# Filler products on TensorE at the start, and batch 1's attention a unit later, in an attention-plus-MLP kernel

## The chip, the cores and the metric

One Trainium2 chip, one core of it, one launch. The time is device microseconds of that core, the median over several runs. Five engines work side by side and are tied by semaphores: TensorE (PE in the profile, its weight loads PEld), VectorE (DVE), ScalarE (ACT), GpSimd (POOL) and SyncE (SP), which issues most of the transfers.

## The reference, cut to what matters

```python
# q, k, v: 8 batches x 8 heads x 576 positions x 64, float32
q_s = exp(q - max(q, axis=-1));  q_s = q_s / (sum(q_s, axis=-1) + 1e-09)
k_s = exp(k - max(k, axis=2));   k_s = k_s / (sum(k_s, axis=2) + 1e-09)
kv  = einsum('bhsd,bhse->bhde', k_s, v)      # 64 x 64 per batch and head
x   = einsum('bhsd,bhde->bhse', q_s, kv)     # then as 4608 tokens x 512
h   = x @ w_in                               # 512 x 2048
out = maximum(0.01 * h, h) @ w_out           # 2048 x 512, float32 out
```

The softmax of q runs over the 64 channels of a position, that of k over the 576 positions of a channel.

## The kernel before, in words

**Two halves of the work.** The attention turns each of the 8 batches into 576 columns of `xT` (512 channels by 4608 tokens, bf16). The two matrix products then run over 9 tiles of 512 tokens: `layer1` (L450) makes 16 blocks of 128 hidden units (four products each, accumulated over the channel blocks in the order 0, 2, 1, 3), `leaky` (L460, ScalarE) writes them as `gj`, and `layer2` (L472) accumulates 16 of them into `pout`, one per 128 tokens; `store` (L465) copies `pout` to `out_sb` and issues two transfers.

**How the order is set.** Nothing is scheduled by a tool: every engine runs its instructions in the order in which the program text issues them. The main loops are cut into units: tile `t` has 16 units for its first layer (one per hidden block) and 16 for its second; tile 0 has 16 units for each half of its tokens in the first layer (0 to 31) and units 32 to 47 in the second layer, one per hidden block with four products each. `at(t, u, ...)` (L484) hangs attention work behind a unit, and `run(t, u)` (L489) issues it there. Batch 0 is done before the first tile; the rest of batch 0 and all of batch 1 hang in tile 0; batch 2 and later ones hang in the tiles that follow.

**The start.** Batch 0's q (rows `RA`, the first four positions of nine of each partition), k and v are loaded first. `wake(n)` (L322) issues n products of a zero tile, 128x512 bf16, into a PSUM bank that nobody reads; 14 of them open TensorE's order. `q_first` (L228) takes the negated maxima of q in two halves on VectorE (`nmax`), and ScalarE makes one exponential with a running sum per head and position. `k_tree` (L149) takes maxima of k on VectorE; `k_max_pe` (L328) transposes them on TensorE, `k_all_dve` reduces, `k_all_pe` (L342) spreads the result over all partitions, and `k_sub_ps` (L352) subtracts. This is done for two pairs of heads in turn, with dummies between the steps. ScalarE then casts v (`v_cast`), and `kv_pair` (L360) multiplies. Four more dummies, `q_transpose` (L386 on), the second `kv_pair`, `attend` (L408), three dummies and the first layer follow. The first weights, `w_in`, come in eight transfers issued by GpSimd (L133) in two groups of four, the second group behind batch 0's subtraction.

**Batch 1's end, in tile 0's second layer.** Behind unit 41 come `kv(1)`, `kd_make(1)` and the transposes of positions 0 to 3; behind unit 43 the transposes of positions 4 to 8, with ScalarE's copies out of PSUM (`q_keep`). Eight `attend` calls, four blocks of channels by two halves of 288 tokens, hang at units 45, 45, 46, 46, 46, 47, 47, 47; ScalarE copies each to `xT`. The four `store` calls of tile 0 are issued after the last unit's products and ahead of what hangs at unit 47 (L666). Tile 1's first layer needs batch 1's columns, and batch 2's maxima (`k_tree`, VectorE) hang at its unit 0, its subtraction at unit 6 and its exponential (ScalarE) at unit 9.

**PSUM.** Two banks hold `pout`; six more (`psB_pool`) are shared by all other tiles, among them the last two `pout2` of tile 0.

Of the kernel before, what the change touches and what calls it, by code (L numbers as in the profile page):

```python
# [8 lines left out]
FP32 = mybir.dt.float32  # L9
# [12 lines left out]
HL = 4  # L22
# [3 lines left out]
def kernel(  # L26
# [9 lines left out]
    nc = tc.nc  # L36
# [10 lines left out]
    P = 128  # L47
    NB = C // P
    NF = F // P
    TT = 512  # L50
    NT = T // TT
    NTS = TT // P
# [9 lines left out]
    small_pool = ctx.enter_context(tc.tile_pool(name="small", bufs=3))  # L62
# [23 lines left out]
    RA, RB = slice(0, 4), slice(4, R)  # L86
    R1, R2 = slice(4, 6), slice(6, R)
    st = [{} for _ in range(B)]
# [15 lines left out]
    identf = const_pool.tile([P, P], FP32)  # L104
# [44 lines left out]
    def k_tree(b, hs, steps=slice(0, 4)):  # L149
        n = hs.stop - hs.start  # L150
        ks = st[b]["k"][:, hs]
        if steps.start == 0:
            st[b]["t4"] = mx_pool.tile([P, HL, 4, D], FP32, name="t4")[:, 0:n]
        t4 = st[b]["t4"]
        t2, t1 = t4[:, :, 0:2], t4[:, :, 0]
        for o, i0, i1 in (
            (t4, ks[:, :, 0:4], ks[:, :, 4:8]),
            (t2, t2, t4[:, :, 2:4]),
            (t1, t1, t4[:, :, 1]),
            (st[b]["kmax"][:, hs], t1, ks[:, :, 8]),  # L160
        )[steps]:
            nc.vector.tensor_tensor(out=o, in0=i0, in1=i1, op=ALU.max)  # L162
# [55 lines left out]
    def q_begin(b):  # L218
        st[b]["qe"] = qe_pool.tile([P, R, HL, D], BF16, name="qe")
        if b < 2:  # L220
            st[b]["qT"] = qT_pool.tile([P, NB, R, L], BF16, name="qT", tag="qT")
# [6 lines left out]
    def q_first(b, rs):  # L228

        n = rs.stop - rs.start  # L230
        nmax = small_pool.tile([P, HL, n], FP32, name="nmax")
        qsum = small_pool.tile([P, n, HL], FP32, name="qsum")
        for hs in (slice(0, 2), slice(2, 4)):
            nc.vector.tensor_reduce(
                out=nmax[:, hs], in_=st[b]["q"][:, hs, rs], axis=AX.X, op=ALU.max, negate=True
            )
            for h in range(hs.start, hs.stop):
                for r in range(n):
                    nc.scalar.activation(
                        out=st[b]["qe"][:, rs.start + r, h],  # L240
                        in_=st[b]["q"][:, h, rs.start + r],
                        func=AF.Exp,
                        bias=nmax[:, h, r : r + 1],
                        accum_out=qsum[:, r, h : h + 1],
                    )
        st[b]["qsum"] = qsum
# [73 lines left out]
    wake_ps = psO_pool.tile([P, TT], FP32, name="pout")  # L320

    def wake(n):  # L322
        for i in range(n):
            nc.tensor.matmul(  # L324
                wake_ps, lhsT=zero[:, 0:P], rhs=zero, start=(i == 0), stop=(i == n - 1)
            )

    def k_max_pe(b, i):  # L328
        ps = psB_pool.tile([P, 2, L], FP32, name="kT", tag=BANK_TAG)
        nc.tensor.matmul(  # L330
            ps.rearrange("c h l -> c (h l)"),
            lhsT=st[b]["kmax"][:, 2 * i : 2 * i + 2].rearrange("p h d -> p (h d)"),
            rhs=identf,
            is_transpose=True,
        )
        st[b]["kT", i] = ps
# [5 lines left out]
    def k_all_pe(b, i):  # L342
        ps = psB_pool.tile([P, P], FP32, name="kallp", tag=BANK_TAG)
        for hh in range(2):
            nc.tensor.matmul(
                ps[hh * L : (hh + 1) * L],
                lhsT=st[b]["kr", i][:, hh : hh + 1].to_broadcast([P, L]),
                rhs=identf,
            )
        st[b]["kallp", i] = ps  # L350

    def k_sub_ps(b, i, hs=slice(0, 2)):  # L352
        ks = st[b]["k"][:, 2 * i + hs.start : 2 * i + hs.stop]
        a = st[b]["kallp", i].rearrange("p (h d) -> p h d", d=D)[:, hs]
        n = hs.stop - hs.start
        nc.vector.tensor_tensor(
            out=ks, in0=ks, in1=a.unsqueeze(2).to_broadcast([P, n, R, D]), op=ALU.subtract
        )
# [26 lines left out]
    def q_transpose(b, r0, n):  # L385
        ps = psB_pool.tile([P, NB, n, L], BF16, name="psum_qt", tag=BANK_TAG)  # L386
        for rr in range(n):
            for gg in range(2):
                nc.tensor.matmul(  # L389
                    ps[:, gg::2, rr],  # L390
                    lhsT=st[b]["qe"][:, r0 + rr, 2 * gg : 2 * gg + 2].rearrange(
                        "p h d -> p (h d)"
                    ),
                    rhs=ident,
                    is_transpose=True,
                    start=(rr == 0 and gg == 0),
                    stop=(rr == n - 1 and gg == 1),
                )
        st[b]["ps", r0] = ps

    def q_keep(eng, b, r0, n, gs=slice(0, 4)):
        o, i = st[b]["qT"][:, gs, r0 : r0 + n], st[b]["ps", r0][:, gs]
        if eng is nc.scalar:
            eng.copy(out=o, in_=i)
        else:
            eng.tensor_copy(out=o, in_=i)

    def attend(b, gs, c0, n, eng):  # L408

        ps = psB_pool.tile([P, len(gs), n], FP32, name="po", tag=BANK_TAG)  # L410
        for i, g in enumerate(gs):
            nc.tensor.matmul(  # L412
                ps[:, i],
                lhsT=kd2[b % 2][:, g],
                rhs=st[b]["qT"][:, g].rearrange("c r l -> c (r l)")[:, c0 : c0 + n],
                start=True,
                stop=True,
            )
        step = gs[-1] - gs[0] if len(gs) == 2 else 1
        o = xT[:, gs[0] : gs[-1] + 1 : step, b * S + c0 : b * S + c0 + n]  # L420
        if eng is nc.scalar:
            eng.copy(out=o, in_=ps)  # L422
        else:
            eng.tensor_copy(out=o, in_=ps)
# [40 lines left out]
    def store(row0, pout, copy=nc.vector.tensor_copy, os=slice(0, O), issue=(nc.sync, nc.sync)):  # L465
        out_sb = osb_pool.tile([P, O], FP32, name="out_sb")[:, os]
        copy(out=out_sb, in_=pout)  # L467
        for i in range(2):
            b, c = divmod(row0 + i * L, S)
            issue[i].dma_start(out=out_r[b, c // L, :, os], in_=out_sb[i * L : (i + 1) * L])  # L470

    def layer2(pout, g_sb, tsub, j, os=slice(0, O)):  # L472
        nc.tensor.matmul(  # L473
            pout,
            lhsT=g_sb[j // 2][:, j % 2, tsub * P : (tsub + 1) * P],
            rhs=w_out_sb[:, j, os],
            start=(j == 0),
            stop=(j == NF - 1),
        )
# [4 lines left out]
    def at(t, u, *fns):  # L484
        while t > 0 and u >= 32:
            t, u = t + 1, u - 32
        hooks.setdefault((t, u), []).extend(fns)

    def run(t, u):  # L489
        for fn in hooks.pop((t, u), ()):  # L490
            fn()

    H0, H1 = slice(0, 2), slice(2, 4)
    GS = (0, 2, 1, 3)
# [12 lines left out]

    HA, HB = slice(0, 1), slice(1, 2)
    wake(14)
    nc.gpsimd.tensor_copy(out=gate[:, 0:1], in_=st[0]["k"][:, HL - 1, R - 1, D - 1 : D])  # L510
    load_w_in(0)
    k_begin(0)
    q_begin(0)
    q_first(0, RA)
    k_tree(0, H0)
    k_max_pe(0, 0)
    wake(1)
    k_tree(0, H1, slice(0, 1))
    k_all_dve(0, 0)
    k_all_pe(0, 0)  # L520
    wake(2)
    k_tree(0, H1, slice(1, 4))
    k_max_pe(0, 1)
# [2 lines left out]
    k_exp(0, slice(0, 1))  # L526
    k_all_dve(0, 1)
    k_all_pe(0, 1)
    wake(2)
    k_sub_ps(0, 0, HB)  # L530
    k_exp(0, slice(1, 2))
    v_cast(nc.scalar, 0, 0)
# [56 lines left out]
    for r0 in (0, 2):  # L589
        at(0, 41, lambda r0=r0: q_transpose(1, r0, 2), lambda r0=r0: q_keep(nc.scalar, 1, r0, 2))  # L590
    for r0, n in ((4, 3), (7, 2)):
        at(0, 43, lambda r0=r0, n=n: q_transpose(1, r0, n), lambda r0=r0, n=n: q_keep(nc.scalar, 1, r0, n))
    for i in range(8):
        at(0, (45, 45, 46, 46, 46, 47, 47, 47)[i], lambda i=i: attend(1, [GS[i // 2]], 288 * (i % 2), 288, nc.scalar))


    XR = (slice(0, 5), slice(5, R))
# [63 lines left out]
    pout = [psO_pool.tile([P, O], FP32, name="pout") for _ in range(2)]  # L661
    pout += [psB_pool.tile([P, O], FP32, name="pout2", tag=BANK_TAG) for _ in range(2)]
    for j in range(NF):
        for tsub in range(NTS):
            layer2(pout[tsub], g_sb, tsub, j)
        if j == NF - 1:  # L666
            for tsub in range(NTS):
                store(tsub * P, pout[tsub])
        run(0, 32 + j)

    for t in range(1, NT):
        g_sb = []
# [54 lines left out]
```

## Time and profile before

| | us |
|---|---|
| median of 3 runs | 294.86 (294.04 to 294.93) |
| the profiled execution | 294.82, of it span 293.0 |
| TensorE busy in the span | 282.1 |
| VectorE, ScalarE, GpSimd busy | 145.6, 150.7, 85.4 |
| TensorE's clock halved | 13.59 to 17.01 |

Times in the profile are microseconds from the start of the span. A row of the timeline gives start, length, engine, line of the kernel, operation, output and inputs, partitions by elements and type, count, and in brackets the idle time of the engine ahead of it with what ended it. A product's length contains the way through the array, so products that follow one another overlap in such rows; their distance is read from the starts. The chain of waits is followed back from the last instruction and names at each step what released it. Line numbers are those of the kernel before.

### The profile page before, as it was taken

Reading aid. Unit: us, or ns where it says so; the run is one execution under the profiler, and the core shown is the slowest. Engines: PE = TensorE matmul, PEld = TensorE weight load, DVE = VectorE, ACT = ScalarE, POOL = GpSimd, SP = SyncE. Lnnn points to the kernel's source line nnn. Section 1 sums busy time; section 2 is a strip of 40 time slices with the busy share of each in tenths; the row PEclk is TensorE's granted clock in tenths of the full one; section 3 lists DMA queues with packets and bytes.
Section 4 is the critical chain, followed back from the end, with each engine's and each line's share of the span. In section 5 each row is a group of like instructions: output and inputs, shape, how many; then the busy total and the mean of one; then the engine's idle time right before and its main releaser. Section 6 shows DMA issues by size and latency. Waiting matters only on the chain.

```text
span 293.0 us, 4282 instructions
## 1 busy us (share of the span) xinstructions
PE 282.1 (96%) x1661; PEld 139.9 (48%) x1661; DVE 145.6 (50%) x240; ACT 150.7 (51%) x272; POOL 85.4 (29%) x61
## 2 busy tenths in 40 slices
PE   8698999999999999999999999999999999999995
PEld 2266845444544455454445544544455444444443
DVE  3946958696592597189367455735440200110011
ACT  4937684678058605951695338532854066007500
POOL 4645190008019307802930292029300000000000
PEclk9989999999999999999999999999999999999999
DMA  7999999496639553774399138933141310131032
GB/s 257 312 216 391 243 181 401 112 287 258 114 76 310 211 116 90 272 266 89 71 309 292 36 72 282 281 74 72 38 81 38 72 36 1 38 72 36 0 72 74
DMA packets 36580, 45.76 MB, mean 156 GB/s; under 512 B 15952, under 2 KB 19280, under 8 KB 36560
## 3 DMA queue, kind: packets, MB, share of 16 engines
q1 hardware_dynamic: 33120, 41.16, 47.9%
q0 software_dynamic: 3280, 4.20, 8.2%
q8 instruction: 13, 0.21, 0.3%
q10 hardware_dynamic: 160, 0.13, 0.1%
q14 instruction: 7, 0.06, 0.1%
HBM read 36.70 MB, written 9.44 MB: 157 GB/s over the span
## 4 chain that ended last, share of the span: by engine, by line
PE 85%; DVE 6%; POOL 2%; ACT 2%; issue 1%; POOLq 0%
PE pout L473 39%; PE ph L452 39%; PE pkv L295 2%; PE po L440 2%; DVE qe L280 1%; DVE qsum L273 1%; POOL k_raw L195 1%; DVE t L162 1%; PE pout L324 1%; PE psum_qt L389 1%; POOL q_raw L256 1%; PE po L412 1%; ACT xT L422 1%; PE pkv L365 1%; ACT qe L264 1%
## 5 line engine op out<-in xcount | busy, mean ns | idle before, releaser
L473 PE MATMUL pout<-w_out_sb,gj 128*128 128x512 bf16 (+2 forms) x592 | 130.4, 373 | 0.0
L452 PE MATMUL ph<-xT,w_in_sb 128*128 128x512 bf16 (+1 forms) x640 | 127.5, 358 | 1.6 <-ACT xT L422 1.6
L461 ACT ACTIVATE gj<-ph 128x512 bf16<-128x512 f32 x144 | 82.3, 604 | 58.1 <-PE ph L452 57.5
L452 PEld LDWEIGHTS <-w_in_sb 128*128 128x128 bf16 x640 | 62.1, 98 | 63.6 <-issue 2.9
L473 PEld LDWEIGHTS <-gj 128*128 128x128 bf16 x592 | 57.0, 98 | 61.8
L467 DVE COPY out_sb<-pout 128x512 f32<-128x512 f32 (+1 forms) x34 | 22.7, 675 | 90.3 <-PE pout L473 84.7
L195 POOL TENSOR_TENSOR k_raw<-k_raw,kall 128x2304 f32<-128x2304 f32 (+1 forms) x6 | 29.1, 4845 | 85.6 <-DVE kall L187 56.9
L256 POOL TENSOR_TENSOR q_raw<-q_raw,qmax 128x2304 f32<-128x2304 f32 (+4 forms) x11 | 31.1, 2836 | 25.8 <-DVE qmax L226 25.8
L273 DVE TENSOR_REDUCE qsum<-qe 128x36 f32<-128x2304 bf16 (+4 forms) x11 | 19.8, 1799 | 37.5 <-ACT qe L264 37.5
L446 ACT CAST xT<-po 128x320 bf16<-128x320 f32 (+1 forms) x48 | 16.8, 402 | 41.2 <-PE po L440 41.2
L203 ACT ACTIVATE ke<-k_raw 128x2304 bf16<-128x2304 f32 (+2 forms) x11 | 17.5, 1595 | 8.9 <-POOL k_raw L195 8.5
L280 DVE TENSOR_TENSOR qe<-qe,qrec 128x2304 bf16<-128x2304 bf16 (+4 forms) x12 | 21.7, 1807 | 0.4
L226 DVE TENSOR_REDUCE qmax<-q_raw 128x36 f32<-128x2304 f32 (+4 forms) x11 | 19.4, 1789 | 0.0
L264 ACT ACTIVATE qe<-q_raw 128x2304 bf16<-128x2304 f32 (+4 forms) x11 | 16.9, 1536 | 0.8 <-POOL q_raw L256 0.8
L215 POOL CAST vb<-v_raw 128x1152 bf16<-128x1152 f32 x12 | 13.4, 1148 | 0.0
L324 PE MATMUL pout<-zero 128*128 128x512 bf16 x27 | 10.5, 536 | 1.3 <-POOL zero L101 1.3
L162 DVE TENSOR_TENSOR t<-k_raw 128x1024 f32<-128x1024 f32 (+1 forms) x10 | 10.1, 1011 | 0.5 <-DMA k_raw<-in_k_dram 0.2
L467 ACT COPY out_sb<-pout 128x512 f32<-128x512 f32 (+1 forms) x3 | 1.7, 550 | 16.2 <-PE pout L473 16.2
L162 DVE TENSOR_TENSOR t<-t 128x256 f32<-128x256 f32 (+2 forms) x20 | 9.6, 478 | 0.6
L440 PE MATMUL po<-qX,kd 128*128 128x320 bf16 (+1 forms) x48 | 9.8, 286 | 0.0
L295 PEld LDWEIGHTS <-ke 64*128 64x128 bf16 x252 | 7.2, 93 | 3.0 <-ACT gj L461 1.7
L313 DVE TENSOR_TENSOR kd<-pkv,krec 64x128 bf16<-64x128 f32 x28 | 8.1, 289 | 0.7
(55 smaller groups left out, 104.2 us busy)
## 6 DMA issues: line engine op xcount, KB each, us to landing
out_dram<-out_sb SPq DMA_DIRECT2D x70, 128.0 KB, 2.4
q_raw<-in_q_dram SPq DMA_DIRECT2D x7, 1152.0 KB, 8.4
v_raw<-in_v_dram SPq DMA_DIRECT2D x7, 1152.0 KB, 11.0
k_raw<-in_k_dram SPq DMA_DIRECT2D x6, 1152.0 KB, 6.0
k_raw<-in_k_dram SPq DMA_DIRECT2D x4, 576.0 KB, 5.8
w_in_sb<-in_moe_w_in_dram POOLq DMA_DIRECT2D x8, 256.0 KB, 6.8
w_out_sb<-in_moe_w_out_dram POOLq DMA_DIRECT2D x3, 512.0 KB, 12.3
v_raw<-in_v_dram SPq DMA_DIRECT2D x2, 576.0 KB, 7.4
```

The lines of the kernel that those rows point to most:

```text
L162: nc.vector.tensor_tensor(out=o, in0=i0, in1=i1, op=ALU.max)
L195: eng.tensor_tensor(out=ks, in0=ks, in1=st[b]["kall"][:, hs].unsqueeze(2).to_broadcast([P, n, R, D]), op=ALU.subtract,)
L203: nc.scalar.activation(out=st[b]["ke"][:, :, hs].rearrange("p r h d -> p h r d"), in_=st[b]["k"][:, hs], func=AF.Exp,)
L226: nc.vector.tensor_reduce(out=m, in_=st[b]["q"][:, :, rs], axis=AX.X, op=ALU.max)
L256: eng.tensor_tensor(out=qs, in0=qs, in1=st[b]["qmax", rs.start].unsqueeze(3).to_broadcast([P, HL, n, D]), op=ALU.subtract,)
L264: nc.scalar.activation(out=st[b]["qe"][:, rs].rearrange("p r h d -> p h r d"), in_=st[b]["q"][:, :, rs], func=AF.Exp,)
L273: nc.vector.reduce_sum(out=qsum, in_=st[b]["qe"][:, rs], axis=AX.X)
L280: nc.vector.tensor_tensor(out=qes, in0=qes, in1=st[b]["qrec", rs.start].unsqueeze(3).to_broadcast([P, n, HL, D]), op=ALU.mult,)
L452: nc.tensor.matmul(ph, lhsT=w_in_sb[:, cb, j * P : (j + 1) * P], rhs=xT[:, cb, c0 : c0 + n], start=(i == 0 and first), stop=(i == NB - 1 a ...
L461: nc.scalar.activation(out=o, in_=ph, func=AF.Prelu, alpha=LEAKY_SLOPE)
L467: copy(out=out_sb, in_=pout)
L473: nc.tensor.matmul(pout, lhsT=g_sb[j // 2][:, j % 2, tsub * P : (tsub + 1) * P], rhs=w_out_sb[:, j, os], start=(j == 0), stop=(j == NF - 1),)
```

## The change

- `wake_on(a, n)` is new: n products of the last head's part of a (128 x 4, float32) with the float32 identity, into the first four partitions of the dummy bank. Four of them follow `q_first`, on `nmax`; they are placed ahead of the first `k_max_pe` in TensorE's order and wait for the maxima.
- The two dummies ahead of the first `kv_pair` become five.
- Batch 1's last two groups of transposes and their copies hang behind unit 44 instead of 43.
- Its eight `attend` calls hang four behind unit 46 and four behind unit 47; ScalarE and VectorE copy them in turn, so four of the eight copies go to VectorE.
- Tile 0's four `store` calls are issued after what hangs at unit 47 instead of ahead of it: in VectorE's order they now follow its four copies of attention results, and SP's eight output transfers come behind them as before.

```diff
-        nmax = small_pool.tile([P, HL, n], FP32, name="nmax")
+        st[b]["nmax"] = nmax = small_pool.tile([P, HL, n], FP32, name="nmax")
...
+    def wake_on(a, n):
+        for i in range(n):
+            nc.tensor.matmul(
+                wake_ps[0:RA.stop, 0:P], lhsT=a[:, HL - 1], rhs=identf, start=True, stop=True
+            )
...
     q_first(0, RA)
+    wake_on(st[0]["nmax"], 4)
     k_tree(0, H0)
...
     k_all_pe(0, 1)
-    wake(2)
+    wake(5)
     k_sub_ps(0, 0, HB)
...
     for r0, n in ((4, 3), (7, 2)):
-        at(0, 43, lambda r0=r0, n=n: q_transpose(1, r0, n), lambda r0=r0, n=n: q_keep(nc.scalar, 1, r0, n))
+        at(0, 44, lambda r0=r0, n=n: q_transpose(1, r0, n), lambda r0=r0, n=n: q_keep(nc.scalar, 1, r0, n))
     for i in range(8):
-        at(0, (45, 45, 46, 46, 46, 47, 47, 47)[i], lambda i=i: attend(1, [GS[i // 2]], 288 * (i % 2), 288, nc.scalar))
+        at(0, 46 + i // 4, lambda i=i: attend(1, [GS[i // 2]], 288 * (i % 2), 288, (nc.scalar, nc.vector)[i % 2]))
...
             layer2(pout[tsub], g_sb, tsub, j)
-        if j == NF - 1:
-            for tsub in range(NTS):
-                store(tsub * P, pout[tsub])
         run(0, 32 + j)
+    for tsub in range(NTS):
+        store(tsub * P, pout[tsub])
```

## The prediction

> **What bounds the kernel now.** I read the page first (span, clock line), then the busy time per stretch, then the timeline of the first 19 us and of 49 to 70 us, and the chain of waits between them. The page:
>
> ```profile
> span 293.0 us, 4282 instructions
> ...
> PEclk9989999999999999999999999999999999999999
> ```
>
> TensorE is busy 282.1 us of the span (the table above), and the third slice of the clock line is an 8: a stretch at a low clock. The next view cuts the span at the clock's own edges, 3.41 us apart; its columns are length, TensorE busy (instructions), clock, DMA share, GB/s:
>
> ```profile
> 6.77:10.18 3.41, 2.16 (x12) 1.00 1.05 388
> 10.18:13.59 3.41, 1.65 (x22) 1.00 1.11 281
> 13.59:17.01 3.42, 3.42 (x32) 0.50 1.12 208
> ...
> 23.83:27.25 3.42, 2.37 (x23) 1.00 1.03 402
> ...
> 30.66:293.00 262.34, 258.44 (x1494) 1.00 0.51 140
> ```
>
> From 13.59 to 17.01 the clock is halved. The stretch ahead of it had TensorE busy 1.65 of 3.41 us (48%); stretches with 2.16 (63%) and 2.37 (69%) were not followed by a drop. After 30.66 the clock stays full and TensorE is idle for only 3.9 us in 262, so whatever the start gains in TensorE's position is kept if nothing later takes it back. TensorE's timeline through the start (start, length, engine, line, operation, count, idle time before and what ended it):
>
> ```profile
> 1.32 5.87 PE L324 MATMUL pout<-zero 128*128 128x512 bf16 x14 [1.32 <-POOL zero L101]
> ...
> 8.11 0.31 PE L330 MATMUL kT<-identf,kmax 128*128 128x128 f32 x1 [0.92 <-POOL gate L510]
> 8.25 0.38 PE L324 MATMUL pout<-zero 128*128 128x512 bf16 x1
> 8.94 0.44 PE L345 MATMUL kallp<-identf,kr 128*64 128x128 f32 x4 [0.31 <-DVE kr L340]
> ...
> 11.16 0.60 PE L324 MATMUL pout<-zero 128*128 128x512 bf16 x2
> 13.21 0.85 PE L365 MATMUL pkv<-vb,ke 64*128 64x129 bf16 x18 [1.45 <-ACT vb L213]
> 13.99 1.89 PE L324 MATMUL pout<-zero 128*128 128x512 bf16 x4
> 15.68 1.06 PE L389 MATMUL psum_qt<-ident,qe 128*128 128x128 bf16 x8
> 16.67 0.83 PE L365 MATMUL pkv<-vb,ke 64*128 64x129 bf16 x18
> 17.43 0.39 PE L412 MATMUL po<-qT,kd 128*128 128x256 bf16 x2
> ...
> 18.50 0.60 PE L452 MATMUL ph<-xT,w_in_sb 128*128 128x256 bf16 x4
> ```
>
> Two holes matter: 0.92 us ahead of 8.11, behind the fourteen opening dummies, and 1.45 us ahead of 13.21. The four dummies at 13.99 are 0.42 apart (15.68 less 13.99, over 4), on the halved clock; on the full one a single dummy takes 0.38 and two take 0.60, so 0.22 apart. ScalarE's rows of the same stretch:
>
> ```profile
> 14.13 1.15 ACT L203 ACTIVATE ke<-k_raw 128x1152 bf16<-128x1152 f32 x1
> 16.77 0.59 ACT L404 COPY qT<-psum_qt 128x512 bf16<-128x512 bf16 x1 [1.50 <-PE psum_qt L389]
> 17.86 0.59 ACT L422 CAST xT<-po 128x512 bf16<-128x512 f32 x1 [0.50 <-PE po L412]
> ```
>
> **The dummies.** Three more ahead of 13.21 cost 3 x 0.22 = 0.66 us and end at about 12.4, inside the hole of 1.45: nothing, while the cast of v still ends it. They lift the stretch before 13.59 from 1.65 to 2.31 busy (68%). A window of 3.41 us laid anywhere between 7 and 14 us then has no more than the 0.8 left of this hole and the 0.3 ahead of the second kallp pair (as ahead of 8.94), about 67%, against 63% that did hold the clock. The four dummies on the negated maxima cannot start before the fourteen end; they fill the hole at 7.2. Each is a 128-column f32 product, which the trace splits in two records. The four f32 records at 8.94 take 0.44 us in all, and one record by itself 0.31 (kT): a new one every 0.04 to 0.11, with two column halves side by side. One after the other that is 0.09 to 0.22 each, 0.7 to 1.8 for eight. Both ends are estimates from these two rows; I take 0.85, near the lower, as the 0.44 contains one record's whole length: done by about 8.05, ahead of the transpose at 8.11. VectorE allows a little more:
>
> ```profile
> 8.00 0.69 DVE L162 TENSOR_TENSOR t<-k_raw 128x512 f32<-128x512 f32 x1
> 8.61 0.28 DVE L340 TENSOR_REDUCE kr<-kT 128x2 f32<-128x128 f32 x1
> ```
>
> The reduction of the transpose starts behind VectorE's own row (8.69), and the transpose was there at 8.42: 0.2 us spare.
>
> **What full clock gives.** Some steps of the chain of waits (start, length):
>
> ```profile
> 21.29 0.61 PE ph L452 x4
> ...
> 23.01 0.53 ACT qe L264
> ...
> 27.48 0.49 PE psum_qt L389 x6
> ...
> 29.32 0.69 DVE xT L424
> ...
> 75.84 1.13 PE pkv L295 x36
> ```
>
> Step by step from 13.21: the eighteen pkv products at the pace of the later 36 in 1.13 us end at 13.78; four dummies at 0.22, 14.65; eight transposes, 1.06 at half clock and so about 0.6, 15.27. ScalarE's exponential ends at 15.28, so it now releases the second pkv group (15.33) and ScalarE's copy of the transposes (15.3 to 15.9). Then po, 15.95 to 16.33; ScalarE's xT, 16.37 to 16.96; first layer at 17.0 instead of 18.50: 1.5 us. The Trainium skill, "TensorE: Matmul & The Clock Gate", section Terms, prices time at a low clock as that time times one less the clock; for these 3.41 us that is an estimate of 1.7, and 293.0 us for the kernel with the same second part. The rows give less, since ScalarE becomes the limit.
>
> What could be late next is w_in, whose last piece of eight is issued at 14.6:
>
> ```profile
> L133 POOL DMA_DIRECT2D w_in_sb<-in_moe_w_in_dram x1: 635/635/635, 14.6 to 14.6; - x1
> ...
> DMA to landing us min/median/max: 7.9/7.9/7.9
> ```
>
> It lands at 22.5. Unit 8's third product needs it; by the row of 21.29 in the chain below that product falls at about 23.25 (16 products of 256 columns, half of 0.22 each, and two more), so 1.5 earlier it would wait 0.75 and TensorE keep 0.75. But the chain does not run through that product. It goes from unit 0 over batch 0's remaining exponentials and VectorE's sums to the transposes at 27.48, for which TensorE waits anyway. So between 0.75 and 1.5, I take 1.4, near the chain's value; all rows up to batch 1's kd move with it.
>
> **The second part: batch 1.** Rows around it, of TensorE, VectorE and ScalarE:
>
> ```profile
> 49.61 0.72 PE L389 MATMUL psum_qt<-ident,qe 128*128 128x128 bf16 x10 [0.29 <-DVE kd L313]
> ...
> 54.60 0.81 PE L452 MATMUL ph<-xT,w_in_sb 128*128 128x512 bf16 x3
> 55.61 13.33 PE L452 MATMUL ph<-xT,w_in_sb 128*128 128x512 bf16 x61 [0.20 <-ACT xT L422]
> ```
> ```profile
> 53.78 2.48 DVE L467 COPY out_sb<-pout 128x512 f32<-128x512 f32 x4 [3.49 <-PE pout L473]
> 56.30 1.23 DVE L162 TENSOR_TENSOR t<-k_raw 128x1024 f32<-128x1024 f32 x1
> ...
> 61.58 2.63 DVE L195 TENSOR_TENSOR k_raw<-k_raw,kall 128x1152 f32<-128x1152 f32 x2
> ```
> ```profile
> 64.28 2.12 ACT L203 ACTIVATE ke<-k_raw 128x2304 bf16<-128x2304 f32 x1
> 66.30 2.05 ACT L461 ACTIVATE gj<-ph 128x512 bf16<-128x512 f32 x4
> 68.21 1.30 ACT L264 ACTIVATE qe<-q_raw 128x1280 bf16<-128x1280 f32 x1
> 69.37 1.11 ACT L461 ACTIVATE gj<-ph 128x512 bf16<-128x512 f32 x2
> ```
>
> A unit later, the last transposes have four more products (0.86) ahead of them: the wait of 0.29 is gone. With two engines copying, the last copy is done 0.1 us earlier than TensorE wants it or 0.15 later (VectorE's 128x512 copy at 29.32 took 0.69, so 288 columns some 0.4), in place of 0.20 late. Gain 0.35 (0.29 to 0.49). The price: the four stores now stand behind VectorE's copies, which need the last products. On the old axis the last products now issue up to 54.3 (54.60 less 0.29), and VectorE's last two copies run from about 54.25 to 55.05. The stores, which started at 53.78, start then: they and the maxima of batch 2 (56.30) come 1.25 later. SP's eight output issues and the loads of batch 3 behind them move as much; batch 3 hangs in later units. But batch 2's exponential at 64.28 follows its subtraction (61.58 and 2.63) at once and stands in ScalarE's line ahead of the last six activations of the tile. Those run without a gap to 70.48, so they end at 71.73. Layer 2 starts at 68.77 (61 products from 55.61 on), now 68.42; its sixteenth weight load is due at about 71.5 (15 x 0.216 less one). TensorE waits 0.2 to 0.3 there; between nothing and 0.6 with the copies' uncertainty. Net of this part: -0.35 + 0.2 = -0.15 (from -0.5 to +0.3).
>
> **Sum.** The profiled execution took 294.82 (span 293.0 and 1.8 around it), the median 294.86, so the same. 294.82 - 1.4 - 0.15 = 293.27: 293.3.
>
> **Rivals.**
> 1. *The clock drops all the same.* What counts as busy is known only from busy shares, and the four small f32 dummies may count for little. Then only part two is left: 294.7. For: one drop at 48% says nothing of 67%; against: 63% and 69% held.
> 2. *The gain is there but partly given back or already in some executions.* If the wait for w_in carries (0.75 kept): 293.9. The clock's edges need not fall alike in every execution: laid from 8.0 the old windows hold 78% and 57% (less the holes of 0.31, 0.32 and 1.45). The three times run from 294.04 to 294.93, so one lacks 0.8 already; the median does not. The Trainium skill, "TensorE: Matmul & The Clock Gate", section Part 1: The HAM clock gate, says the window is free-running and the ramp varies from run to run; the 3.41 spacing agrees, and no single trace shows the rest.
> 3. *VectorE's late stores cost more.* If ScalarE's backlog costs the whole 1.25 instead of 0.2: 294.82 - 1.4 - 0.35 + 1.25 = 294.3.
> 4. *Slower: the f32 dummies hold up the transpose.* If their eight records don't overlap, at 0.31 each (kT's row) they run from 7.2 to 9.7, 1.55 late; less 0.2 spare, 1.35 on the whole chain, and the hole that drops the clock comes later with it: 294.82 + 1.35 - 0.15 = 296.0. It decides from a delay of about 1.2 us on. Against: four such records took 0.44 together.
>
> **Chances.** Forecast 0.52, with its own range 292.8 to 293.8; rival 1, 0.20; rival 2, 0.12, of which two thirds beyond the bound; rival 3, 0.08; rival 4, 0.08. Within 0.3% (0.88 us, about what a measurement here can tell) of 294.86 lie rivals 1, 3 and a third of 2. Faster 0.6, same 0.32, slower 0.08. The range 292.8 to 294.8 leaves out rival 4 and the edges.
>
> **What would show it.** Right: no 0.50 in the clock between 13 and 17 us, the first layer's first product near 17.0, a wait for w_in near 22, psum_qt without its 0.29, a TensorE wait on gj near 70. Wrong: the clock still halved in any stretch before 20 us; kT after 8.3; k_raw's maxima of batch 2 so late that ScalarE's activations stop layer 2 for more than half a microsecond.

## The result, and the profile after

| | before | after |
|---|---|---|
| median of 16 runs | 294.18 (from 293.85) | 293.34 (from 293.14) |
| ratio after/before | | 0.9962, 95% interval 0.9945 to 0.9979 |
| the profiled execution | 294.82 | 293.27 |
| its span | 293.0 | 291.5 |

The change makes the kernel 0.4% faster, with an interval from 0.2 to 0.55%; the ratio weighs all runs, the two medians alone give 0.9971. The forecast was 293.3. The gain between the two profiled executions is 1.55 us, as forecast; between the medians it is 0.84. That difference is the subject of the first experiments. Lines of the changed kernel carry numbers six higher from the new function on (first layer L458, second L479, stores L473).

The page of the changed kernel: no 8 in the clock line any more.

```profile
span 291.5 us, 4277 instructions
...
PEclk9999999999999999999999999999999999999999
```

Busy time per stretch, cut at this execution's own clock edge (5.79, where the clock first rises) and every 3.41 us after it; columns as in the prediction's table:

```profile
5.79:9.21 3.42, 2.42 (x14) 1.00 1.05 398
9.21:12.62 3.41, 3.02 (x17) 1.00 1.09 330
12.62:16.03 3.41, 2.43 (x44) 1.00 1.12 208
16.03:19.45 3.42, 3.39 (x35) 1.00 1.12 192
19.45:22.86 3.41, 2.17 (x19) 1.00 1.11 240
22.86:26.27 3.41, 2.79 (x26) 1.00 1.04 385
```

The edges lie elsewhere than in the trace before (6.77, 10.18, 13.59). Up to 16 us no stretch is under 71% busy (2.42 of 3.42). The lightest is now 19.45 to 22.86, with 64%. TensorE's timeline shows why:

```profile
6.63 1.04 PE L330 MATMUL pout<-identf,nmax 128*4 128x128 f32 x8
8.34 0.33 PE L336 MATMUL kT<-identf,kmax 128*128 128x128 f32 x1 [0.67 <-DVE kmax L162]
...
11.49 1.25 PE L324 MATMUL pout<-zero 128*128 128x512 bf16 x5
13.54 0.68 PE L371 MATMUL pkv<-vb,ke 64*128 64x129 bf16 x18 [0.80 <-ACT vb L213]
...
15.03 0.61 PE L395 MATMUL psum_qt<-ident,qe 128*128 128x128 bf16 x8
15.66 0.69 PE L371 MATMUL pkv<-vb,ke 64*128 64x129 bf16 x18
...
17.37 1.91 PE L458 MATMUL ph<-xT,w_in_sb 128*128 128x256 bf16 x16
...
23.44 1.69 PE L458 MATMUL ph<-xT,w_in_sb 128*128 128x256 bf16 x14 [1.15 <-DMA w_in_sb<-in_moe_w_in_dram]
...
26.35 0.49 PE L395 MATMUL psum_qt<-ident,qe 128*128 128x128 bf16 x6
```

The four f32 dummies take 1.04 us in all and the transpose behind them waits for its own input, VectorE's maxima. The five dummies end inside the hole, of which 0.80 is left. The first layer starts at 17.37 instead of 18.50, although q's first transfer came 0.33 later in this execution (VectorE's first maxima start at 4.98 against 4.65): counted from q's arrival it is 1.46 us earlier. The transpose at 8.34 lies just beyond the prediction's sign of being wrong (kT after 8.3); it is the later input that puts it there, for it still waits 0.67 us for the maxima when the dummies are done. Then TensorE waits 1.15 for w_in, and at 26.35 it is ahead of the trace before (27.48) by 1.13 again.

Around the end of batch 1, ScalarE's and TensorE's rows and TensorE's weight loads:

```profile
64.16 2.12 ACT L203 ACTIVATE ke<-k_raw 128x2304 bf16<-128x2304 f32 x1 [1.44 <-DVE k_raw L195]
```
```profile
48.88 0.72 PE L395 MATMUL psum_qt<-ident,qe 128*128 128x128 bf16 x10
...
53.30 13.97 PE L458 MATMUL ph<-xT,w_in_sb 128*128 128x512 bf16 x62
67.11 7.16 PE L479 MATMUL pout<-w_out_sb,gj 128*128 128x512 bf16 x32
```
```profile
70.42 1.62 PEld L479 LDWEIGHTS <-gj 128*128 128x128 bf16 x9 [0.39 <-ACT gj L467]
```

The transposes come without their wait of 0.29, the first layer runs without its wait of 0.20, and ScalarE idles 1.44 us ahead of batch 2's exponential. Of that a wait of 0.39 arrives at one weight load of layer 2.

### The profile page after: what moved, and what is told of

The parts are those of the page before. It is cut to its first block, busy times and chain, and to the rows that moved or that the text cites. A ratio compares the mean times of both kernels' runs of the same rounds, so it can differ in the third digit from the quotient of the medians.

```text
span 291.5 us, 4277 instructions
## 1 busy us (share of the span) xinstructions
PE 280.2 (96%) x1645; PEld 139.9 (48%) x1672; DVE 147.0 (50%) x244; ACT 149.7 (51%) x268; POOL 85.5 (29%) x61
## 4 chain that ended last, share of the span: by engine, by line
PE 89%; DMA 3%; DVE 1%; issue 1%; ACT 1%; POOL 1%; ACTq 0%
PE pout L479 43%; PE ph L458 41%; DMA w_in_sb<-in_moe_w_in_dram 3%; PE pkv L295 3%; PE po L446 2%; DVE k_raw L362 1%; PE psum_qt L395 1%; POOL w_in_sb L133 0%; ACT gj L467 0%; ACT xT L428 0%; PE po L418 0%; DVE out_sb L473 0%; POOL gate L542 0%; ACTq L467 0%
## 5 line engine op out<-in xcount | busy, mean ns | idle before, releaser
L479 PE MATMUL pout<-w_out_sb,gj 128*128 128x512 bf16 (+2 forms) x580 | 129.6, 373 | 0.6
L458 PE MATMUL ph<-xT,w_in_sb 128*128 128x512 bf16 (+1 forms) x626 | 126.8, 357 | 3.4 <-ACT xT L428 1.4
L458 PEld LDWEIGHTS <-w_in_sb 128*128 128x128 bf16 x640 | 62.1, 98 | 64.8 <-issue 4.1
L479 PEld LDWEIGHTS <-gj 128*128 128x128 bf16 x592 | 57.0, 98 | 62.1 <-ACT gj L467 0.4
L473 DVE COPY out_sb<-pout 128x512 f32<-128x512 f32 (+1 forms) x34 | 22.7, 675 | 86.2 <-PE pout L479 80.7
L324 PE MATMUL pout<-zero 128*128 128x512 bf16 x29 | 9.6, 470 | 1.5 <-POOL zero L101 1.3
L473 ACT COPY out_sb<-pout 128x512 f32<-128x512 f32 (+1 forms) x3 | 1.7, 563 | 14.9 <-PE pout L479 14.9
```

Source lines behind the costliest of these rows:

```text
L458: nc.tensor.matmul(ph, lhsT=w_in_sb[:, cb, j * P : (j + 1) * P], rhs=xT[:, cb, c0 : c0 + n], start=(i == 0 and first), stop=(i == NB - 1 a ...
L479: nc.tensor.matmul(pout, lhsT=g_sb[j // 2][:, j % 2, tsub * P : (tsub + 1) * P], rhs=w_out_sb[:, j, os], start=(j == 0), stop=(j == NF - 1),)
```

## The experiments

Times below are medians of a kernel's runs. A drop is a stretch of 3.41 us at half clock, an edge is a point where such a stretch can begin. Each execution also comes with its mean clock: 1.00 to 0.997 where the clock stays full from its first rise to the last products (the traces show it halved again behind them, from 290.86 in the run with the four dummies alone, 0.998), 0.994 or 0.993 with one drop (1.7 of 292), 0.988 to 0.983 with two or more. That sorts executions without a trace of each.

**Where the kernel before stands.** In the three comparisons below it ran 85 times. Of these 79 (six above 296 us, all with a drop, left out) lie in two groups: 49 from 293.64 to 294.54 and 30 from 294.64 to 295.48. The cut is made by hand; the two at 294.64 and 294.65 could belong to the low group. The low group has 18 executions without a drop (median 293.92) and 31 with one (294.11); the high one has 13 with one (295.06) and 17 with two (295.36). The profiled execution, 294.82, was of the high group. The drop that it shows is priced about rightly in the prediction, but most executions don't pay that price.

**The dummies alone.**

```diff
+    wake_on(st[0]["nmax"], 4)      # and the function, and nmax kept, as in the change
...
-    wake(2)                        # ahead of the first kv_pair
+    wake(5)
```

> Only the dummies of the change (four on q's maxima, three more ahead of the first pkv group); batch 1 as before. Theory A (the dummies stop the drop of the clock, worth 1.4 us, and batch 1's part is worth 0.15): no clock of 0.50 in the profile, 293.4 in every execution, against 294.8 of the kernel before where its clock drops. Rival B (the clock of the kernel before drops only in executions whose windows fall badly, and batch 1's part is worth about 0.6): all executions near 293.9, where the undisturbed ones of the kernel before lie, so that the median gains little. Rival C (the dummies do nothing): the same two groups of times as the kernel before, 293.9 and 294.9.

Measured: 293.75 (293.59 to 294.05, 12 runs), no drop in any; before beside it 294.29, ratio 0.9973 (0.9959 to 0.9988). The times are rival B's: all executions stand where the undisturbed ones of the kernel before stand (293.92), a little lower. Theory A's mechanism holds too, as every drop is gone; its 293.4 was too low, because it starts from the profiled 294.82, which is 0.24 under the median of the executions like it (295.06). Rival C falls. Two rows of the trace serve below as the measure for batch 1's part:

```profile
26.32 0.50 PE L395 MATMUL psum_qt<-ident,qe 128*128 128x128 bf16 x6
...
67.61 7.07 PE L479 MATMUL pout<-w_out_sb,gj 128*128 128x512 bf16 x32
```

**Batch 1's part alone.**

```diff
-        at(0, 43, ... q_transpose(1, r0, n) ...)
+        at(0, 44, ... q_transpose(1, r0, n) ...)
-        at(0, (45, 45, 46, 46, 46, 47, 47, 47)[i], ... nc.scalar ...)
+        at(0, 46 + i // 4, ... (nc.scalar, nc.vector)[i % 2] ...)
...                                 # and the stores behind unit 47
```

> Only batch 1's part (transposes behind unit 44, copies in turn, stores behind them); start as before. Theory A: 0.15 us less than the kernel before, group by group: 293.75 without a drop, 294.65 with one. Rival B: 0.6 less: 293.3 without a drop, about 294.3 with one; the drop still there in some executions. In both the wait of 0.29 ahead of the transposes is gone, and ScalarE waits some 1.3 us for batch 2's subtraction ahead of its exponential.

Measured: 294.32 (12 runs), ratio 0.9997 (0.9977 to 1.0017): nothing that can be told, since the drops spread its times. Ten of twelve executions had one; the two without took 293.05 and 293.51, 0.4 to 0.9 under the undropped 293.92 of before. That is rival B's 0.6 rather than theory A's 0.15, from two executions. In its trace the wait of 0.29 is gone and ScalarE idles 1.44 us ahead of the exponential, as expected. The trace shows a drop at another place (stretches, then two rows of TensorE):

```profile
5.15:8.56 3.41, 1.24 (x6) 1.00 1.04 405
8.56:11.98 3.42, 3.41 (x14) 0.50 1.07 376
11.98:15.39 3.41, 2.05 (x27) 1.00 1.13 216
```
```profile
8.57 0.45 PE L330 MATMUL kT<-identf,kmax 128*128 128x128 f32 x1 [2.18 <-POOL gate L510]
...
17.90 1.91 PE L452 MATMUL ph<-xT,w_in_sb 128*128 128x256 bf16 x16
```

The edge at 5.15 lets the opening dummies end at 6.4, so the first hole is over 2 us (36% busy) and the drop comes early. The first layer then starts at 17.90, with the halved stretch behind it, instead of 18.50, although q came 0.47 later: an early drop costs less than a late one.

**One sort of dummies each.** First the three ahead of the first pkv group only, then the four on q's maxima only.

```diff
-    wake(2)
+    wake(5)
```

> Of the change only the three more dummies ahead of the first pkv group. Theory A: they fill the stretch that had 48% busy to 67% and are enough by themselves wherever the clock rises at the first full window: no drop, as the kernel with both sorts of dummies. Rival D (the hole at 7.2 us counts as much): drops remain in some executions, and the median lies between.

Measured: 294.22 (12 runs), ratio 0.9991 (0.9970 to 1.0011). Nine executions had a drop, seven of them between 293.93 and 294.39, two with lower clock means at 295.1 and 295.2. Theory A's "no drop" falls; rival D's drops remain. Its profile, of 293.93, drops early, behind the hole that is left open:

```profile
6.39:9.80 3.41, 1.64 (x10) 1.00 1.05 392
9.80:13.21 3.41, 3.41 (x12) 0.50 1.11 309
```

```diff
+    wake_on(st[0]["nmax"], 4)
```

> Of the change only the four f32 dummies on q's maxima. Theory A: the stretch with 48% busy is untouched, so the drop stays as often as in the kernel before: groups at 293.9 and 294.9. Rival D: the drop is gone, as with both sorts. If the four hold up the transpose behind them (rival 4 of the prediction), the undisturbed group is later than 293.9 by that.

Measured: 294.43 (12 runs), ratio 0.9996 (0.9974 to 1.0017). Six executions have no drop, 293.58 to 293.85; six have one, 295.02 to 295.26, and there is nothing between. The medians of the two groups, 293.73 and 295.09, differ by 1.36: the price of the drop behind the second hole, 1.4 in the prediction. (That these six drop there is inferred from the hole left open; the profiled execution has none.) Here it is theory A's two groups that came, and rival D's "gone" that did not. The two runs together say what neither theory said: each hole has its own drop, and only both sorts together keep the clock up. Four f32 dummies don't hold up the transpose: the undropped group isn't late, and in its trace the transpose waits 0.90 us for VectorE's maxima when they are done.

**The second hole opened wider**, in the changed kernel.

```diff
-    wake(5)
+    wake(0)
```

> The changed kernel without any of the five dummies ahead of the first pkv group: the hole there grows from 0.8 to 1.9 us, and the worst window of 3.41 us holds 36% busy or so. If the busy share of a window decides (theory A with rival B's edges): a drop between 12 and 15 us in more of the executions than in the kernel before with its 48%, that is in more than half, at 1.4 us each: most times near 294.7, the rest near 293.3. If a drop needs TensorE idle for about a whole window: none.

Measured: 295.16 (12 runs) against 294.64 of the kernel before and 293.27 of the changed one beside it. Ten of twelve have a drop, six of these two. The profiled one (295.45):

```profile
8.82:12.24 3.42, 1.96 (x12) 1.00 1.08 354
12.24:15.65 3.41, 2.22 (x21) 0.50 1.12 209
15.65:19.06 3.41, 3.41 (x31) 0.50 1.12 209
```

The reading by busy share holds, with more drops than it forecast; that a drop needs TensorE idle for a whole window falls, as the longest idle time here is 1.98 us. So five dummies that compute nothing are worth 1.9 us of median here. In this trace a stretch at half clock with 65% busy (2.22) wasn't enough to bring the full clock back; the next, full one was.

**Does it matter that four dummies wait for q?**

```diff
-    wake(14)
+    wake(18)
...
-    wake_on(st[0]["nmax"], 4)
```

> The changed kernel with the four f32 dummies replaced by four more zero dummies at the opening, which wait for nothing. Where the clock rises early, these are done up to 0.5 us sooner than the four that wait for q's maxima, and leave up to 1.5 us idle ahead of the transpose. Theory A: the early drop (8 to 10 us at its start, worth some 0.3 to 0.6) comes back in few executions or none, and the median stays within 0.2 of 293.3. Rival G (the wait for the maxima is what matters): early drops in a good part of the executions, median 293.6 or more.

Measured: 293.37 (8 runs), no drop in any; the changed kernel beside it 293.27. No difference that could be told in eight runs, so rival G falls; whether an early edge would show one is open.

**The price of the late stores.** Batch 2's exponential two units later:

```diff
-        at(1, 9, lambda: k_exp(b, ALLH))
+        at(1, 11, lambda: k_exp(b, ALLH))
```

> The changed kernel with batch 2's exponential behind unit 11 of tile 1 instead of unit 9, so that ScalarE doesn't idle 1.44 us ahead of it. Theory A (the late stores cost TensorE only what it waits on gj at the start of layer 2, about 0.1): ScalarE's idle time and TensorE's wait on gj are gone, 0.1 us less than the changed kernel, 293.2. Rival E (the late stores cost more, further back): 0.3 or more less.

Measured: 293.27 (12 runs), the changed kernel beside it 293.35. The difference of 0.08 is theory A's, and less than the runs can tell; rival E falls. ScalarE's idle time is gone, as its row without a wait shows. Layer 2's weight load still waits 0.29 for gj, against 0.39, but layer 2 again takes 7.00 to batch 2's pkv instead of 7.09. One of the twelve took 295.69, and it is the profiled one: ScalarE's row, a line of TensorE's waits (total, times, longest), and two stretches.

```profile
66.86 2.12 ACT L203 ACTIVATE ke<-k_raw 128x2304 bf16<-128x2304 f32 x1
```
```profile
PE ph L458 <- DMA w_in_sb<-in_moe_w_in_dram: 2.0, 2, 1.8
```
```profile
22.28:25.70 3.42, 1.50 (x13) 1.00 1.05 371
25.70:29.11 3.41, 3.41 (x23) 0.50 1.05 396
```

Here the wait for w_in itself is the hole: 2.0 us, a stretch with 44% busy, and a drop at 25.70.

**The stores back ahead of the last four products**, all else as changed:

```diff
+        if j == NF - 1:
+            for tsub in range(NTS):
+                store(tsub * P, pout[tsub])
         run(0, 32 + j)
-    for tsub in range(NTS):
-        store(tsub * P, pout[tsub])
```

> The changed kernel with the four stores back ahead of the last four attention products, all else as changed. VectorE then runs 2.5 us of stores ahead of its last two copies: tile 1's first layer waits some 2.2 us for them, and batch 2's chain is late by 0.8 as well. Theory A: about 295.5. Rival F (the order of the stores doesn't matter): 293.3.

Measured: 294.96 (12 runs, no drop in any), 1.6 above the changed kernel. The first layer of tile 1 waits for VectorE's copy (VectorE's stores, then TensorE):

```profile
52.15 2.47 DVE L473 COPY out_sb<-pout 128x512 f32<-128x512 f32 x4
```
```profile
55.04 13.71 PE L458 MATMUL ph<-xT,w_in_sb 128*128 128x512 bf16 x62 [1.36 <-DVE xT L430]
```

Rival F falls. The expected wait of 2.2, and with it 295.5, was too high: VectorE starts the stores at 52.15, before the last products. With copies on VectorE, the stores have to stand behind them.

**Can w_in come earlier?** First the second half without its gate, then batch 1's loads held one piece longer (the latter with batch 2's exponential behind unit 11 too).

```diff
-    nc.gpsimd.tensor_copy(out=gate[:, 0:1], in_=st[0]["k"][:, HL - 1, R - 1, D - 1 : D])
     load_w_in(1)
```

> The changed kernel without the gate that holds w_in's second half behind batch 0's subtraction: it is issued right behind the first half, some 2.3 us earlier. The wait of 1.15 us for w_in goes or shrinks to nothing. If the advance runs past that wait, as the prediction had it: the same time, 293.3, within 0.1. If w_in carries the chain, as the chain of waits of the changed kernel has it: up to 0.5 less. If the earlier transfer delays v or the rest of q, the first pkv group is late by that and the time longer.

```diff
-    hold_sync(0, w_in_sb[0:1, 0, F - 128 : F])
+    hold_sync(0, w_in_sb[D : D + 1, 0, F - 128 : F])
```

> The kernel with batch 2's exponential behind unit 11, and batch 1's loads held until the second piece of w_in's second half has landed instead of the first (1.3 us later). The last pieces of w_in then have less beside them: TensorE's wait for w_in shrinks from 1.1 to 0.7 or less. If w_in still carries the chain: 0.1 to 0.3 less than the changed kernel, 293.1. If VectorE's sums end that stretch anyway (they were level with TensorE at 26.2 us): 0.1 less, all of it from the exponential. If batch 1's k comes too late for its maxima at 28 us: slower by that.

Measured: 293.26 (9 runs) and 293.25 (6 runs); the changed kernel beside them 293.35 and 293.27. Neither did what it was made for: TensorE's wait for w_in was 1.6 and 1.5. Without the gate the last piece is issued at 12.5 and takes 11.2:

```profile
L133 POOL DMA_DIRECT2D w_in_sb<-in_moe_w_in_dram x2: 653/658/664, 11.9 to 12.5; - x2
...
DMA to landing us min/median/max: 10.6/10.9/11.2
```

It lands at 23.7, no sooner than with the gate (23.3): what limits it is the moving of the data, not the issue. So in no run did w_in land earlier. But the traces bound what that could give. In the first repetition of the changed kernel (below), where TensorE waits only 1.07 for w_in, it is VectorE's sums that end the next wait (VectorE, then TensorE):

```profile
25.33 0.96 DVE L280 TENSOR_TENSOR qe<-qe,qrec 128x768 bf16<-128x768 bf16 x1
```
```profile
26.44 0.50 PE L395 MATMUL psum_qt<-ident,qe 128*128 128x128 bf16 x6 [0.21 <-DVE qe L280]
```

TensorE's transposes start 0.15 after VectorE's end there. In the traces without a drop where the wait for w_in is 1.42 to 1.55 they start 0.14 to 0.26 after it, while VectorE's end lies 21.20 to 21.23 after q's arrival in all of them. So an earlier w_in would give about 0.1 us at most, as long as its wait drops no clock.

**The changed kernel again**, beside the two sets of variants:

> The changed kernel itself, beside three variants of it on one chip. One group of times near 293.3, no drop of the clock in any execution: the busy share of no window of 3.41 us falls under 65%.

> The changed kernel itself, beside three more variants on one chip: 293.3, with a drop of the clock in none or one execution.

Measured: 293.35 (11 runs), ratio 0.9966 (0.9952 to 0.9981), and 293.27 (6 runs), ratio 0.9949 (0.9930 to 0.9968). No drop in these 17; one in the 16 of the result (295.33, mean clock 0.994). Over 33 executions that is one, against 67 of 85 in the kernel before. "No window under 65%" was wrong: the trace of the second repetition holds the clock through one with 55%, at the wait for w_in:

```profile
21.65:25.06 3.41, 1.86 (x18) 1.00 1.03 330
```

## Why the prediction was right

*The time, 293.3.* It came out at 293.34, and the two profiled executions differ by the forecast 1.55. That it fits this closely is partly luck. The sum starts from an execution that was itself early: its q arrived at 4.65, in the other thirteen traces at 4.76 to 5.17, and the executions like it have a median 0.24 higher (295.06). Batch 1's part, on the other hand, was taken 0.26 too small. With the measured terms the sum is 295.06 - 1.36 - 0.41 = 293.29; the two errors cancel. What failed outright is the sentence on the median: "the median 294.86, so the same" took the one traced drop for the rule. It is rival 2's second half, that the edges need not fall alike, which is right about the kernel before; its chance of 0.12 was far too small. About half of the gain is therefore missing between medians: 30 of 79 executions lie in the high group, the others have an early drop, worth 0.2 to 0.6 by the groups of before and of the three dummies alone, or none. The three times shown, one of them 0.8 lower, were the sign.

*The dummies.* Right in mechanism. Three more cost nothing (the five end 0.80 ahead of the pkv group), the four f32 ones took 1.04 against 0.85, and the transpose is not held up; rival 4 falls with the undropped group of the four alone. Rival 1 falls with no drop in 12 executions of the dummies alone. What the prediction did not see is that the four matter as much as the three: it gave the first hole no drop of its own, and it has one, by edges that the trace before did not have.

*What full clock gives, 1.4.* Measured 1.36 between the groups of the four dummies alone. The traces say it most sharply: from q's arrival to the first layer's start it takes 12.37 to 12.40 us in the ten traces without a drop ahead of it, and 13.85 in the kernel before, 1.46 more. In the traces with an early drop it takes 12.78 (batch 1's part alone) and 12.51 (three dummies alone), in that with two stretches in a row (the second hole opened wider) 14.68. One reason that the gain stays under half of 3.41 is that ScalarE releases the next steps once TensorE is faster, as the weight loads of the second pkv group in the changed kernel show:

```profile
15.66 0.51 PEld L371 LDWEIGHTS <-ke 64*128 64x128 bf16 x18 [0.19 <-ACT ke L203]
```

The Trainium skill, "TensorE: Matmul & The Clock Gate", section Terms, takes the time at a low clock times one less the clock, for this stretch an estimate of 1.7. The runs say less, 1.36 to 1.46. The Trainium skill, "TensorE: Matmul & The Clock Gate", section Part 1: The HAM clock gate, says that the window is free-running and does not start with the kernel. The traces here agree: the clock first rises between 4.14 and 7.01 us in fourteen profiled executions, and every drop among their products lasts one or two times 3.41.

*The wait for w_in.* Right in place, too small in size: 0.75 forecast, 1.07 to 2.0 in the profiles, since the last piece lands at 23.3 or later. The 22.5 of the trace before, on which the forecast rests, is the earliest of all fourteen traces; why it is, isn't shown. That the chain does not run through it was right in effect: TensorE's lead is gone at 23.44 and back at 26.35, where VectorE's sums end (26.20). They are level there, and the chain of waits of the changed kernel now names w_in; no more than 0.1 us hangs on it. That this wait is long enough to drop the clock by itself was not foreseen; it is the likely place of the one drop in 33 executions, which cost 2 us, but no trace shows that one.

*Batch 1's part, -0.15.* The mis-sized term. Beside the dummies alone (293.75, measured in another comparison), the whole change takes 293.34: -0.41. Both waits are gone entirely, 0.29 and 0.20, where I took 0.35 of their 0.49. In the traces layer 2 of tile 1 starts 0.50 earlier than with the dummies alone (67.11 against 67.61, with the transposes at 26.35 and 26.32). Of the price, 0.2 forecast, 0.09 arrives: from layer 2's start to batch 2's pkv it takes 7.09 instead of 7.00. The mechanism (stores late by their place behind VectorE's copies, ScalarE idle at the exponential, a wait on gj) is in the trace at each step, so rival 3 falls.

## What to carry to other kernels

A profile shows one position of the clock's edges. Before a low-clock stretch is priced into a median, sort the runs' times into groups and ask which holes could drop the clock with other edges; fill them all: here filling one alone moved the median by less than the runs can tell (ratios 0.9991 and 0.9996), because the edges found the other. And work that starts earlier for a full clock may meet a transfer that does not: that wait is the next hole.

## What the runs showed of the hardware

The busy share that drops the clock is not a sharp number in this profile. Ahead of 34 us, stretches with 36, 44, 48, 48 and 57% busy were followed by a drop; one that reads 52% was held in the run with the four dummies alone,

```profile
10.97:14.38 3.41, 1.78 (x25) 1.00 1.16 245
```

and so were several with 55 to 59%. Neither the length of a hole nor its place between two edges decides alone. A hole of 1.45 us inside one stretch was followed by a drop in the kernel before and with the three dummies alone; one of 1.44, also inside one stretch, was held with the four dummies alone. A hole of 1.55 at the wait for w_in was held in the second repetition of the changed kernel, and one of 1.98 that an edge cuts in two (at 12.24, in the run with the second hole opened wider) was followed by a drop.

Part of the blur is in the profile. First, in the stretch of 52% the record of one product is missing: there are four weight loads of the dummies and three products (TensorE, then its weight loads).

```profile
14.26 0.81 PE L324 MATMUL pout<-zero 128*128 128x512 bf16 x3 [0.16 <-issue]
```
```profile
14.03 0.55 PEld L324 LDWEIGHTS <-zero 128*128 128x128 bf16 x4
```

With it the share is about 57%. Second, a product's length contains its way through the array: a single dummy lasts 0.38 us, and the next starts 0.22 later, so about 0.16 at the end of every run of products is no new work. With these 0.16 taken off each product's end (an estimate from the starts and lengths in the traces), the five stretches ahead of a drop hold 32, 36, 36, 39 and 40%, and every stretch up to 34 us that was held has 43% or more. One stretch near the end of a kernel (288.72 to 292.13 in the run with the second hole opened wider) has 39% and was held too, so even this is no exact measure, and no run was made to test it.

The profile's clock reads 1.00 ahead of the first rise, where the opening dummies are still 0.43 apart: that part of the clock line says nothing.
